# Loads of the first pairs, multiplies and the passage of a convolution and maxout kernel in another order

## The chip, the cores and the metric

The kernel runs on one NeuronCore of a Trainium2 chip. The metric is the time of one execution on the device, in microseconds (us). Before the change it is 2294.14 us, the median of three runs (2293.34 to 2296.65).

## The reference

A long convolution feeds a feed-forward block with three parallel input products. Shapes: B = 4 batches, S = 12544 positions, D = 128 channels, 50176 tokens in all, 768 hidden units; everything is float32.

```python
h_mlp = np.maximum(pos_emb @ w1, 0.0) @ w2
h_filt = h_mlp * np.exp(-0.01 * np.arange(S))[:, None]
u = x * v
Uf = np.fft.rfft(u, n=2 * S, axis=1)
Hf = np.fft.rfft(h_filt, n=2 * S, axis=0)
y = np.fft.irfft(Uf * Hf[None], n=2 * S, axis=1)[:, :S, :]
t = (x * y).reshape(B * S, D)
h = np.maximum(np.maximum(t @ moe_w1, t @ moe_w2), t @ moe_w3)
out = h @ moe_w_out
```

## The kernel before

The Fourier transform is done as products with small tables on TensorE (PE), in three steps. A first step takes 32 units of four channels each (`unit`, line 427, through `u_first`, L413) and leaves a spectrum of 90 columns in one large buffer, `spec`. A second step goes through 45 pairs of columns: each pair is transformed, multiplied with the spectrum of the filter, and transformed back half way. The results are rows, kept in device memory as `zd`. The third step belongs to the output: a tile of four positions per channel loads its rows (`t_load`), adds and subtracts their two halves (`t_sums`), and multiplies them with the table f4p and with x (`t_last`).

The instructions stand in the order in which the program text issues them (the schedule is manual). Each engine takes its own instructions strictly in that order, and so does SP, the engine that issues most of the DMAs. A DMA also waits until the DMA that stood eight places earlier in its queue has landed, because eight completion counters are used in turn.

**Three stages.** The opening (0 to about 308 us) convolves batch 0 and makes the filter. The middle (to about 1830 us) computes the feed-forward block of batch b - 1 and, beside it, the convolution of batch b, for b = 1, 2, 3. The end does the feed-forward block of batch 3 alone.

**The middle** counts time in slots. A batch has NT = 32 output tiles of NF = 6 hidden blocks, so 192 slots, each about 2.7 us of PE work. `conv_steps(b, done)` gives every step of the convolution a slot, and the main loop runs the steps of a slot after that slot's own work. Within one slot the loop first does `up` (two products into the banks hps, a Relu on ACT at L745, a maximum on DVE at L748), then the z sums of a coming tile, then the steps.

A unit u of the convolution passes through five steps. `u_load` (SP) fetches x and v. `u_mul` multiplies them on GpSimd, which the profile calls POOL (L361). `u_planes` clears the padding of a planes tile on POOL (L381) and copies the product there on ACT (L382). `u_dma` transposes it by a DMA from SP (L388). `u_join` puts the halves together on ACT (L397). Then `unit` runs on PE. With s the slot of the join, the load stands at s - 9, the multiply at s - 6, the planes at s - 5 and the transpose at s - 4. For batch 1 the first six units are done in the opening, and slots below zero are not used; for batches 2 and 3 the first units start in the last slots of the batch before.

A pair g has two loads. `q_load` (L443) regroups the spectra `sq` of two pairs out of `spec`, from on-chip memory to on-chip memory, four DMAs of 128 KB each. `h_load` (L456) loads the filter rows `ht` of two pairs from `hd` in device memory, four DMAs of 256 KB each. `w_load` (L433) loads one table. `g_quarter` multiplies them on PE (L472 forward, L482 back), and `q_re` on DVE (L516) is the first to read `ht`. The first pairs start at slot 55 in batch 1 and at slot 59 in batches 2 and 3; loads start no earlier than slot 52 (`LOADS`), because their buffers take the place of the buffers of the first eight tiles, whose output stores (L833, on SP) must be issued first.

**The passage** is what this text calls 285 to 326 us, between the opening and the middle. In its loop a step s transforms pair s, makes filter s - 1 (`s_filter`, ACT copy L1050 into `ht`), stores filter s - 2 (`s_store`, POOL, L1056) and multiplies pair s - 2 with it (`g_re`, `g_im`; for pair 43 the last add, L559, is on POOL). Pairs 43 and 44 come together at s = 45. `g_unfold` (DVE, L566) gives the operand `ab` of `g_third` (PE), whose copy `zs` is stored to `zd` by SP (L579). Then come units 0 and 1 of batch 1, the product of two weight matrices (`fold`), the constants f4p and sign, weight differences `tw` on POOL (L1136), and the first two output tiles. The PSUM banks of units 0 and 1 and of two transposes are given out by `banks_of`; before, the two halves of unit 1 share one tile of two banks.

Of the kernel before, what the change touches and what calls it, by code (L numbers as in the profile page):

```python
# [10 lines left out]
FP32 = mybir.dt.float32  # L11
# [5 lines left out]
P = 128  # L17
# [74 lines left out]
def kernel(  # L92
# [15 lines left out]
    nc = tc.nc  # L108
    NG, _, _, B, NB = x.shape
# [4 lines left out]
    NK = N1 // 2  # L114
# [10 lines left out]
    zd = [dram.tile([N1, 2, 64, 256] if b == 0 else [N1, 2, 32, 2, 256], FP32, name=f"zd{b}")  # L125
          for b in range(B)]
# [4 lines left out]
    f4p_d = nc.inline_tensor(np.ascontiguousarray(f4p_t), name="f4p_const").ap()  # L131
# [3 lines left out]
    sign_d = nc.inline_tensor(sign.copy(), name="sign_const").ap()  # L135
# [446 lines left out]
    def conv_steps(b, done):  # L582


        out = []

        def at(slot, late, fn, *args):
            out.append((slot, late, len(out), fn, args))

        for u in range(4, done):
            at(2 * (u - 4), 1, unit, u)
        lead, low = (1, -NT * NF) if b > 1 else (6, 0)
        share = UNIT * (NU - done - 1)
        per_pair = (END - lead - 6) / (share + (NK + LATE) // 2 * 2 - 2)
        for u in range(done, NU):
            s = (u - done) * UNIT * per_pair + lead
            load_ = max(low, int(s) - 9)
            at(load_, 0, u_load, b, u)  # L600
            mul = max(load_ + 2, int(s) - 6)
            at(mul, 0, u_mul, u, nc.gpsimd)
            at(max(mul, int(s) - 5), 0, u_planes, u)
            at(max(mul + 1, int(s) - 4), 0, u_dma, u)
            at(int(s), 0, u_join, u)
            at(int(s + 1), 1, unit, u)
        s0 = int(share * per_pair + lead) + 6

        def start(x):
            return s0 + int(x // 2 * 2 * per_pair)  # L610

        load = [0.6] * (NT * NF)
        for x in range(NK + LATE):
            s = start(x)
            load[s] -= 1.2
            load[s + 1 + x % 2] += 1.4

        def emptiest(among, cost):
            s = min(among, key=lambda i: load[i])
            load[s] += cost  # L620
            return s

        plan = []
        busy = {start(x): 2 for x in range(NK + LATE)}
        for x in range(NK + LATE):
            busy.setdefault(start(x) + 1, 1)
        for i in range(NT - 1):
            s = i * NF
            last = min((3, 4, 2), key=lambda k: busy.get(s + k, 0))
            load[s + last] += 0.6  # L630
            if s <= s0:
                plan.append((0, 0, last))
                continue
            a = emptiest(range(s, s + 2), 0.7) - s
            plan.append((a, emptiest(range(s + a, s + max(a + 1, last - 1)), 0.7) - s, last))
        plan.append((3, 3, 4))

        for x in range(NK + LATE):
            s, odd = start(x), x % 2
            g, z = x if x < NK else None, x - LATE if x >= LATE else None  # L640
            at(s, 1, g_quarter, g, z)
            at(s + 1 + odd, 0, g_fold, g, z)
            at(max(s - 4, LOADS) if x > 2 else LOADS + x // 2, 0, w_load, x)
            if z is not None:
                at(s + 3 + odd, 0, g_store, b, z)
            if g is None:
                continue
            if g % 2 == 0:
                at(max(s - 4, LOADS), 0, q_load, g, min(2, NK - g))
                at(s - 1 if g > 2 else LOADS + 1 + g // 2, 0, h_load, g, min(2, NK - g))  # L650
            first = s + 2 + 2 * odd
            at(first, 0, q_swap, g, 0)
            at(first + 1, 0, q_swap, g, 64)
            last = start(x + LATE) - 1
            a = emptiest(range(first + 1, min(first + 3, last - 1) + 1), 0.7)
            at(a, 0, q_re, g)
            a = emptiest(range(a, min(first + 4, last - 1) + 1), 0.7)
            at(a, 0, q_im, g)
            two = sorted(emptiest(range(a + 1, last + 1), 0.55) for _ in range(2))
            for q in range(2):  # L660
                at(two[q], 0, q_unfold, g, q)
        slots = {}
        for s, _, _, fn, args in sorted(out, key=lambda r: r[:3]):
            slots.setdefault(s, []).append((fn, args))
        return slots, plan, s0
# [5 lines left out]
    LOADS = TP * NF + 4  # L671
    UNIT, END = 0.65, 178
    zts, xTs, gs, pos_, obs = ({} for _ in range(5))

    def t_load(b, i):
        zt = hp.tile([N1, 2, 512], FP32, tag="zt", name="zt", bufs=2)
        for c in range(2):
            if b == 0:
                nc.sync.dma_start(
                    zt[NK * c:NK * c + NK],  # L680
                    zd[b].rearrange("(g a) c t f -> g a c t f", a=2)[
                        :, :, c, 2 * i:2 * i + 2, :].rearrange("g a t f -> g a (t f)"))
                continue
            q, j = divmod(i, NT // 2)
            for a in range(2):
                nc.sync.dma_start(
                    zt[NK * c:NK * c + NK, a].rearrange("g (t f) -> g t f", t=2),
                    zd[b].rearrange("(g a) c t q f -> g a c t q f", a=2)[
                        :, a, c ^ (a & q), 2 * j:2 * j + 2, q, :])
        zts[b, i] = zt[:, 0], zt[:, 1]  # L690
        if i % 2:
            return
        xT = hp.tile([D, 2, 4, NB], FP32, tag="xT", name="xT", bufs=2)
        for c in range(GC):
            nc.sync.dma_start(xT[c * NG:(c + 1) * NG].rearrange("d i p n -> d (i p) n"),
                              x[:, 4 * i:4 * i + 8, c, b, :])
        xTs[b, i], xTs[b, i + 1] = xT[:, 0], xT[:, 1]
# [248 lines left out]
    for f in range(0, FO, 4):  # L946
        quad([hs[:, f + i] for i in range(4)], (f1h[:, 0], f1h[:, 1]), specH[:, :, :, f:f + 4])
        u, k = divmod(f // 4, 4)
# [11 lines left out]
    for u in range(0, NU, 2):  # L960
        t = uts.pop(u)
        for v in range(2):
            if u + 4 < NU:
                u_mul(u + 4 + v)
            at = 4 * (u + v)
# [18 lines left out]
    cps = pro.enter_context(tc.tile_pool(name="cps0", bufs=3, space=PSUM))  # L984
    gps = pro.enter_context(tc.tile_pool(name="gps", bufs=2, space=PSUM))
    sps = pro.enter_context(tc.tile_pool(name="sps", bufs=1, space=PSUM))
    def banks_of():
        for _ in range(2):
            yield gps.tile([P, 512], FP32, tag="g", name="ps1")[:]
        both = sps.tile([P, 1024], FP32, tag="h", name="ps1")  # L990
        for h in range(2):
            yield both[:, 512 * h:512 * h + 512]
        for pool, tag in ((cps, "cv"), (gps, "g")):
            yield pool.tile([P, 512], FP32, tag=tag, name="pst")

    free = banks_of()

# [56 lines left out]
    def s_store(g):  # L1054
        for c in range(2):
            nc.gpsimd.dma_start(  # L1056
                hd[g, 64 * c:64 * c + 64],
                hts[g][64 * c:64 * c + 64, c].rearrange("p k q d -> p (k q d)"))
# [13 lines left out]
    for s in range(NK + 3):  # L1072
        if s < NK:
            ws[s, 0] = wf[s]
            s_second(s)
            if s + 1 < NK:
                s_minus(s + 1)
            g_second(s)
            wf.pop(s)
            if s + 3 < NK:  # L1080
                wf[s + 3] = load_dir(s + 3, 0)
        if 1 <= s <= NK:
            g_swap(s - 1)
            s_filter(s - 1)
        if s >= 3:
            ws[s - 3, 1] = wi.pop(s - 3)
            g_third(s - 3)
            if s < NK:
                wi[s] = load_dir(s, 1)
        ready = [g for g in {NK: (s - 2, s - 1)}.get(s, (s - 2,)) if 0 <= g and s <= NK]  # L1090
        for g in ready:
            s_store(g)
            g_re(g)
            g_im(g, g == NK - 2)
        for g in ready:
            g_unfold(g)
        if s < NK:
            g_butterfly(s)

        if s in muls:  # L1100
            u_mul(muls[s])
        if s in turns:
            u_turn(turns[s])
        if s in loads:
            u_load(1, loads[s])
        if s == NK:
            unit(0)
            pl = sps.tile([P, 512], FP32, tag="pl", name="pl")
        if s == NK + 1:
            for f in range(2):  # L1110
                folding(f)
# [11 lines left out]
    hidp = ctx.enter_context(tc.tile_pool(name="hidp", bufs=3))  # L1123
    hp = ctx.enter_context(tc.tile_pool(name="hp", bufs=3))
    f4p = hp.tile([N1, 2, 2, NB // 2], FP32, name="f4p", bufs=1)
    nc.sync.dma_start(f4p[:], f4p_d)
    sign_t = hp.tile([N1, 1], FP32, name="sign", bufs=1)
    nc.sync.dma_start(sign_t[:], sign_d)
    tw = hp.tile([P, 4, NC, 64], FP32, name="tw", bufs=1)
    linx = hp.tile([D, 64], FP32, name="linx", bufs=1)  # L1130
    b11, b12 = wo_sb[:, 0:NC, 0:64], wo_sb[:, 0:NC, 64:128]
# [34 lines left out]
    for n, (b, i) in enumerate(tiles[:LAST]):  # L1166
# [13 lines left out]
        for f in range(NF):  # L1180
            s = i * NF + f
# [130 lines left out]
```

## Time and profile before

| what | value |
|---|---|
| median of three runs | 2294.14 us |
| profiled execution | 2290.28 us |
| its span | 2288.5 us |
| mean granted PE clock | 0.995 |
| busy: PE, DVE, ACT, POOL | 99%, 68%, 54%, 44% of the span |
| DMA | 411.15 MB, mean 180 GB/s |
| issue to landing, median: ht, sq, wt | 6.6, 6.9, 5.8 us |

The profile is of one execution. Its span runs from the first to the last instruction of the program, and the execution's own time is 1.8 us longer. All times within it are counted from the start of the span. A timeline row gives the start, the length, the engine, the line, the operation and its tiles, and in brackets how long the engine had been idle before and what released it. SPq is SP's queue: the length of a row there is the time in which SP issues, and the transfer lands later. Busy time of PE is that of pipelined matmuls with modelled ends, so a busy PE is not always a fast one.

### The profile page before, as it was taken

What the parts mean: (1) busy time and instruction counts of PE and PEld (TensorE: products, weight loads), DVE (VectorE), ACT (ScalarE), POOL (GpSimd) and SP (SyncE); (2) the same over time, 40 slices, a digit from 0 to 9 for tenths busy, and PEclk for the clock granted to TensorE, in tenths of its full rate; (3) what the DMA queues carried; (4) which work ended last, traced back from release to release, by engine and by line L of the source; (5) the groups of instructions that cost most, each with busy time, mean ns of one, the idle gap of its engine ahead of it and who ended that gap; (6) DMA issues with size and microseconds to landing.
All of it is one profiled execution on the core that took longest, in us unless ns stands there. A gap on an engine that the chain in (4) does not pass through costs nothing.

```text
span 2288.5 us, 70172 instructions
## 1 busy us (share of the span) xinstructions
PE 2254.5 (99%) x28383; PEld 1397.2 (61%) x28383; DVE 1545.8 (68%) x3108; ACT 1227.9 (54%) x2210; POOL 1004.3 (44%) x1209
## 2 busy tenths in 40 slices
PE   8999989999999999999999999999999999999998
PEld 7999857745555557755555557755555556666665
DVE  5588956657878756658888856658888854545443
ACT  2688845546666546546666646536666622222222
POOL 2044357513333347713333348713333326666666
PEclk9999999999999999999999999999999999999999
DMA  7779979789999789979999889968999832222221
GB/s 192 178 238 276 300 168 185 129 197 233 234 242 236 201 161 188 168 168 232 247 239 235 225 151 193 171 160 229 246 243 236 216 86 56 55 67 66 61 55 23
DMA packets 485567, 411.15 MB, mean 180 GB/s; under 512 B 341305, under 2 KB 387866, under 8 KB 485242
## 3 DMA queue, kind: packets, MB, share of 16 engines
q1 hardware_dynamic: 459778, 334.30, 65.5%
q0 software_dynamic: 24752, 70.65, 10.3%
q8 instruction: 223, 3.65, 0.7%
q10 hardware_dynamic: 712, 1.70, 0.3%
q14 instruction: 102, 0.84, 0.1%
HBM read 262.84 MB, written 84.67 MB: 152 GB/s over the span
## 4 chain that ended last, share of the span: by engine, by line
PE 94%; DMA 3%; issue 1%; SPq 1%; POOL 0%; ACT 0%; DVE 0%; POOLq 0%; ACTq 0%; DVEq 0%
PE hps L156 43%; PE ops L156 14%; PE ops L809 8%; PE cps L413 5%; PE ps L156 4%; PE cps L156 4%; PE cps L472 3%; PE ps L165 3%; PE cps L482 3%; PE cps L809 2%; PE sps L1045 2%; PE gps L1027 2%; PE last L156 1%; DMA zt<-zd 1%; DMA sq<-spec 1%
## 5 line engine op out<-in xcount | busy, mean ns | idle before, releaser
L156 PE MATMUL hps<-gt,w_sb 128*64 128x392 f32 x6144 | 1147.7, 495 | 2.0 <-ACT hid L745 1.9
L745 ACT ACTIVATE hid<-hps 128x392 f32<-128x392 f32 x768 | 382.2, 498 | 822.5 <-PE hps L156 794.6
L748 DVE TENSOR_TENSOR hid<-hid,hps 128x392 f32<-128x392 f32 x768 | 428.1, 558 | 433.7 <-PE hps L156 331.1
L156 PEld LDWEIGHTS hps<-gt,w_sb 128*64 128x64 f32 x6144 | 419.9, 137 | 420.3 <-issue 387.1
L524 POOL TENSOR_TENSOR cb<-cb,xs 128x512 f32<-128x512 f32 x135 | 175.2, 1297 | 458.2 <-DVE xs L521 362.9
L156 PE MATMUL ops<-hid,wo_sb 128*64 128x392 f32 x1728 | 358.1, 493 | 0.0
L497 DVE TENSOR_TENSOR cb<-cps,eo 128x512 f32<-128x512 f32 (+1 forms) x288 | 175.1, 649 | 72.8 <-ACT eo L494 72.8
L156 PEld LDWEIGHTS ops<-hid,wo_sb 128*64 128x64 f32 x1728 | 124.5, 137 | 160.2 <-issue 160.1
L763 POOL DMA_DIRECT2D out_dram<-ot x72 | 56.7, 787 | 287.5 <-ACT ot L761 212.3
L512 ACT ACTIVATE xs<-cb 32x512 f32<-32x512 f32 x270 | 169.5, 628 | 19.4 <-DVE cb L497 10.5
L513 ACT COPY xs<-cb 32x512 f32<-32x512 f32 x270 | 166.3, 616 | 3.2
L528 DVE TENSOR_TENSOR xs<-cb 128x256 f32<-128x256 f32 x270 | 143.1, 575 | 9.3 <-POOL cb L524 9.3
L413 PE MATMUL cps<-f1q,uT 98*64 98x90 f32 x3008 | 133.6, 241 | 1.8 <-ACT uT L397 1.2
L413 PEld LDWEIGHTS cps<-f1q,uT 98*64 98x64 f32 x3008 | 127.2, 137 | 11.6 <-ACT uT L397 4.4
L397 ACT COPY uT<-turned 98x512 uint16<-98x512 uint16 x180 | 127.5, 781 | 0.0
L505 POOL DMA_DIRECT2D zd<-cb x135 | 92.5, 685 | 64.1 <-DVE cb L497 61.2
L778 POOL TENSOR_TENSOR s<-hid 128x392 f32<-128x392 f32 x84 | 86.4, 1028 | 75.1 <-DVE hid L748 73.8
L425 DVE TENSOR_TENSOR spec<-cps,high 128x180 f32<-128x180 f32 x376 | 112.6, 341 | 6.4
L778 POOL TENSOR_TENSOR s<-hid,s 128x392 f32<-128x392 f32 x84 | 86.4, 1029 | 49.8 <-DVE hid L748 49.4
L156 PEld LDWEIGHTS cps<-f4p,even 90*64 90x64 f32 x1568 | 87.9, 138 | 30.2 <-issue 29.2
L423 DVE COPY high<-cps 128x180 f32<-128x180 f32 x188 | 89.9, 478 | 23.2 <-PE cps L413 21.8
L361 POOL TENSOR_TENSOR ut<-ut 128x392 f32<-128x392 f32 x90 | 92.2, 1024 | 29.2 <-DMA ut<-in_vr_dram 26.4
(148 smaller groups left out, 3490.7 us busy)
## 6 DMA issues: line engine op xcount, KB each, us to landing
ht<-hd SPq DMA_DIRECT2D x264, 256.0 KB, 6.6
wt<-wq_const SPq DMA_DIRECT2D x144, 256.0 KB, 5.8
zd<-cb POOLq DMA_DIRECT2D x135, 256.0 KB, 5.4
zt<-zd SPq DMA_DIRECT2D x384, 90.0 KB, 3.1
sq<-spec SPq DMA_DIRECT2D x264, 128.0 KB, 6.9
ut<-in_xr_dram SPq DMA_DIRECT2D x128, 196.0 KB, 4.0
ut<-in_vr_dram SPq DMA_DIRECT2D x128, 196.0 KB, 4.1
xT<-in_x_dram SPq DMA_DIRECT2D x256, 98.0 KB, 3.3
```

Of the source, the lines that this page charges most:

```text
L156: nc.tensor.matmul(out[64 * h:64 * h + 64], lhsT[:, 64 * h:64 * h + 64], rhs, start=start, stop=stop, skip_group_check=True)
L397: nc.scalar.copy(uts[u][:, 8 * (u % 2):8 * (u % 2) + 8].rearrange("n s r t -> n (s r t)").bitcast(U16).rearrange("n (s r t h) -> n h s r t ...
L413: nc.tensor.matmul(ps[64 * c:64 * c + 64, 256 * i + h * N1:256 * i + (h + 1) * N1], t[:, 2 * ((at + i) % 8) + h].rearrange("n r t -> n (r ...
L497: nc.vector.tensor_tensor(out=cb[:, a, lo:hi], in0=ps[0][:, lo:hi], in1=eo[:, lo:hi], op=op)
L512: nc.scalar.mul(xs[at:at + 32], xt[at + 32:at + 64], -1.0)
L513: nc.scalar.copy(xs[at + 32:at + 64], xt[at:at + 32])
L524: nc.gpsimd.tensor_tensor(out=xts[g], in0=xts[g], in1=xs[:], op=ALU.add)
L528: nc.vector.tensor_tensor(out=ab[:, q], in0=y[:, 0], in1=y[:, 1], op=(ALU.subtract, ALU.add)[q])
L745: nc.scalar.activation(h[:], pa[:, 0:N], Relu)
L748: nc.vector.tensor_tensor(out=h[:], in0=h[:], in1=pb[:, 0:N], op=ALU.max)
L778: nc.gpsimd.tensor_tensor(out=out[:], in0=a[:], in1=b[:], op=op)
L809: nc.tensor.matmul(ps[64 * c:64 * c + 64, 0:H2], w, rhs[:, H2 * c:H2 * c + H2], start=start, stop=True, skip_group_check=True)
```

## The change

Five edits are made.

1. `conv_steps`: the multiply moves from slot s - 6 to s - 7, and the planes stand at least one slot after it. The transpose stands one slot after the planes. For the first three units of batch 1 this changes slots: units 6 and 7 keep the multiply at slot 2 and get planes at 3 and transpose at 4 (before 2 and 3); unit 8 gets its multiply at slot 2 (before 3).
2. `conv_steps`: the filter rows of the first two loads (g = 0 and 2) are loaded at s - 1, as all later ones are. Before they stood at slots 53 and 54; now at 54 and 59 in batch 1 and at 58 and 63 in batches 2 and 3.
3. The first z tile is loaded in two parts: 43 of the 45 row pairs, then the last two.
4. `banks_of` gives the two halves of unit 1 different tiles.
5. In the passage, stores of filters 42, 43 and 44 stand one step earlier or ahead of the multiplications, and f4p and sign are loaded from POOL's queue instead of SP's.

```diff
-            mul = max(load_ + 2, int(s) - 6)
+            mul = max(load_ + 2, int(s) - 7)
             at(mul, 0, u_mul, u, nc.gpsimd)
-            at(max(mul, int(s) - 5), 0, u_planes, u)
-            at(max(mul + 1, int(s) - 4), 0, u_dma, u)
+            planes = max(mul + 1, int(s) - 5)
+            at(planes, 0, u_planes, u)
+            at(planes + 1, 0, u_dma, u)
...
-                at(s - 1 if g > 2 else LOADS + 1 + g // 2, 0, h_load, g, min(2, NK - g))
+                at(s - 1, 0, h_load, g, min(2, NK - g))
...
+    def load_rows(zt, i, c, lo, hi):
+        nc.sync.dma_start(
+            zt[NK * c + lo:NK * c + hi],
+            zd[0].rearrange("(g a) c t f -> g a c t f", a=2)[
+                lo:hi, :, c, 2 * i:2 * i + 2, :].rearrange("g a t f -> g a (t f)"))
+
...
-                nc.sync.dma_start(
-                    zt[NK * c:NK * c + NK],
-                    zd[b].rearrange("(g a) c t f -> g a c t f", a=2)[
-                        :, :, c, 2 * i:2 * i + 2, :].rearrange("g a t f -> g a (t f)"))
+                load_rows(zt, i, c, 0, NK if i else NK - 2)
...
+        if b == i == 0:
+            for c in range(2):
+                load_rows(zt, i, c, NK - 2, NK)
...
-        for _ in range(2):
-            yield gps.tile([P, 512], FP32, tag="g", name="ps1")[:]
-        both = sps.tile([P, 1024], FP32, tag="h", name="ps1")
-        for h in range(2):
-            yield both[:, 512 * h:512 * h + 512]
-        for pool, tag in ((cps, "cv"), (gps, "g")):
-            yield pool.tile([P, 512], FP32, tag=tag, name="pst")
+        for pool, tag, n in ((gps, "g", 1), (gps, "g", 1), (sps, "h", 2), (gps, "g", 1),
+                             (cps, "cv", 1), (gps, "g", 1)):
+            yield pool.tile([P, 512 * n], FP32, tag=tag, name="ps1")[:, 0:512]
...
+        for g in {NK - 2: (s - 2, s - 1), NK - 1: (s - 1,), NK: (s - 1,)}.get(s, (s - 2,)):
+            if 0 <= g and s <= NK:
+                s_store(g)
         for g in ready:
-            s_store(g)
             g_re(g)
...
-    nc.sync.dma_start(f4p[:], f4p_d)
+    nc.gpsimd.dma_start(f4p[:], f4p_d)
...
-    nc.sync.dma_start(sign_t[:], sign_d)
+    nc.gpsimd.dma_start(sign_t[:], sign_d)
```

## The prediction

> **What bounds the kernel.** I read the page first, then TensorE's waits, then the granted clock around each wait, then the queues that ended it. The page:
>
> ```profile
> span 2288.5 us, 70172 instructions
> PE 2254.5 (99%) x28383; PEld 1397.2 (61%) x28383; DVE 1545.8 (68%) x3108; ACT 1227.9 (54%) x2210; POOL 1004.3 (44%) x1209
> ```
>
> TensorE (PE) is busy in all but 34 us, so a change that adds no matmul can gain only from those 34 us and from time in which PE is busy but slow. The waits of PE (releaser, sum, count, longest) name the 34:
>
> ```profile
> PE cps L472 <- DMA sq<-spec: 7.9, 7, 3.0
> PE ps L156 <- DVE ab L566: 4.3, 1, 4.3
> PE hps L156 <- ACT hid L745: 1.9, 2, 1.0
> PE ps L413 <- DVE spec L425: 1.3, 1, 1.3
> ```
>
> The 7.9 us are waits for the spectra of the first pairs. By PE's timeline they lie at 469.68 (0.17), 482.91 (2.99) and 486.34 (0.94) in the convolution of batch 1, 1001.41 (1.69) and 1003.54 (0.24) in batch 2, 1517.89 (1.38) and 1519.70 (0.47) in batch 3. The other three rows are the passage (285 to 326 us). The busy table of short windows, with the columns PE, PEld, DVE, ACT, POOL, clock, DMA share, GB/s, shows what follows a wait:
>
> ```profile
> 483.40:486.81 3.41, 0.43 (x4) 0.22 (x4) 2.62 (x5) 0.01 (x1) 0.62 (x1) 1.00 1.01 218
> 486.81:490.22 3.41, 2.94 (x44) 2.33 (x44) 0.00 (x0) 0.00 (x0) 0.64 (x1) 0.50 1.19 199
> 490.22:493.64 3.42, 3.42 (x16) 1.26 (x14) 0.34 (x1) 0.50 (x1) 0.00 (x0) 0.50 1.03 250
> 1521.04:1524.46 3.42, 3.42 (x16) 1.24 (x12) 0.18 (x1) 0.76 (x2) 0.00 (x0) 0.50 0.73 166
> 302.49:305.90 3.41, 3.41 (x18) 2.24 (x18) 0.55 (x2) 1.31 (x5) 0.00 (x0) 0.50 0.47 132
> ```
>
> After an idle window PE runs at half clock for one or two more, so a wait costs more than its length.
>
> **What the skill says.** The Trainium skill, "TensorE: Matmul & The Clock Gate", section "What's actually happening": the clock is full or half, by activity in free-running windows of 3413 ns. The trace agrees in the length (3.41 and 6.83 us at 0.50). It drops to half after an idle window there; here a window with 2.08 of 3.42 us busy (299.07 on) was enough, and I use that. "DMA: Bandwidth & Descriptors", section "Issuing engines are not separate DMA queues": DMAs of all engines run on the same 16 DMA engines and interleave. This agrees: spectra issued alone at 464.43 landed 3.6 us later, spectra issued at 476.14 behind rows took some 9. "SBUF — State Buffer", section "Who interferes with whom": a VectorE (DVE) instruction with two SBUF inputs contends with a GpSimd (POOL) one that reads SBUF. In the passage the DVE add L559 took 1.73 us beside POOL's subtractions, 0.69 elsewhere.
>
> **Part A, the row loads ht of the first pairs** (3 batches, two loads of four DMAs each, 256 KB a DMA by the page's issues). SP's timeline before:
>
> ```profile
> 472.09 3.03 SPq L456 DMA_DIRECT2D ht<-hd  x4
> 476.14 3.30 SPq L443 DMA_DIRECT2D sq<-spec  x4
> ...
> 482.54 2.04 SPq L679 DMA_DIRECT2D zt<-zd  x2
> ```
>
> In the built order of batch 1 the second ht load goes behind the second sq load. By bytes from 463.9 on, ahead of the end of that sq load stand three wt (0.75 MB), two sq (1.0), one zt (0.18), one ht (1.0) and an output tile (0.2): 3.13 MB. At the 220 GB/s of this stretch that is 14.3 us, from the first landing's start near 466: landed at about 480.5, and PE comes at 482.91. The wait goes. What is late next: the first ht, at about 478.5, wanted by DVE at 479.56; and the third sq load, which stays near 495 as the DMA engines are full (1.01 to 1.19), wanted by PE at 503.55 less what was gained, about 496. Both just hold. In batches 2 and 3 both ht loads leave the front of the first sq load. Spectra are complete at 991.50 (DVE's last L425), the sq load issues then and lands within 6 us, at 997.5; PE comes at 1001.41. Gain: 7.9 - 0.17 = 7.7 us of waits; half-clock time, half of it lost: (2.94 + 3.42 + 3.42)/2 = 4.9. **A = -12.6**, bounds -13.5 and -5.5.
>
> **Part P, the passage.** Of the filter stores, the built order of POOL moves one: the store of filter 44 now stands ahead of POOL's add L559 of pair 43. It waits for ACT's ht copy, ending 289.45; the add moves from 287.03 to about 290.85 and ends at 292.1, which is when DVE's L566 needs it (292.47). The 4.3 us wait therefore stays (0, bounds +0.5 and -0.3; DVE's L559 now meets this add instead of the subtractions). The banks: the second half of unit 1 no longer shares a tile with the first, so the 1.3 us wait goes (-1.3), and the half clock of 302.49 loses its cause, worth at most 3.41/2 = 1.7 (I take -0.7). The z load in two parts costs two more issues on SP (up to 0.9 us each by the rows of zt) and starts 43 of 45 rows at 300.0 instead of 301.86; its second part waits for the last zd stores (landed 301.78), with the xT and the second z load behind it as before; ready near 305 instead of 306.4. It hides behind PE's folds until 308.86 before; with PE about 2 us earlier it just holds, but the second z tile (landed near 309.4, two sums of 0.69 us) then holds PE some 0.5 (+0.5). The f4p and sign loads cost SP nothing, since they stood inside its wait for the last zd store (299.61 to 301.78); on POOL two issues of 0.54 us delay the tw subtractions, which nobody needs before 336. **P = -1.5**, bounds -3.0 and +0.5.
>
> **Part C, the multiplies.** 93 muls of 1.02 us, none added. Many wait for their load already (POOL ut <- DMA), so a slot (2.7 us) earlier they wait longer, with sums, stores and memsets queued behind. PE has no wait on any of these between 330 and 464, so this is hidden: a transpose lands mostly 4 us or more before its join. The exception is the start of batch 1, where units 6 and 7 lose a slot of planes:
>
> ```profile
> 318.99 1.02 POOL L361 TENSOR_TENSOR ut<-ut 128x392 f32<-128x392 f32 x1
> 319.95 0.30 POOL L381 MEMSET planes<- 128x240 uint16 x1
> 320.21 1.03 POOL L361 TENSOR_TENSOR ut<-ut 128x392 f32<-128x392 f32 x1
> 321.17 0.30 POOL L381 MEMSET planes<- 128x240 uint16 x1
> 321.43 1.26 POOL L710 TENSOR_TENSOR even<-zt 90x512 f32<-90x512 f32 x1
> 322.76 1.27 POOL L710 TENSOR_TENSOR zt<-zt 90x512 f32<-90x512 f32 x1
> ```
>
> The built order after is three muls, both z sums, then the memsets. The third mul's load (issued 316.87, to landing up to 5.5; SP some 0.6 ahead of before) comes near 321.8, mul to 322.9, sums to 325.4, first memset to 325.7, transpose landed 3.7 to 3.9 us later at 329.5, two join copies of 1.43 together: unit 6 starts at 331.0, not 329.28. Behind the waiting join on ACT stand the next planes copy and the next hid, behind the waiting third mul on POOL the z sums and all memsets. The two ACT hid waits (1.9) disappear, so PE arrives at 327.4 and stands 3.6 us. Net +1.7, and such a stand brings one or two half-clock windows, 1.7 each (I take 2.4). **C = +4.1**, bounds -0.3 (early loads, no half clock) and +6.3.
>
> **Sum.** -12.6 - 1.5 + 4.1 = -10.0. The profiled execution took 2290.28 us (span 2288.5), 3.9 under the median of 2294.14; I take the difference off the median: 2284.
>
> **Rivals.** (1) It goes better: the loads land early and C is at its low end, P too: -12.6 - 3.0 - 0.3 = -15.9, 2278. For it: landings of 3.2 us occur. Against: two z sums stand ahead whatever lands. (2) Batch 1's wait stays, since the DMA engines and not the order set it (share 1.0 and over): only batches 2 and 3 gain, 3.78 + 1.7 = 5.5; -5.5 - 1.5 + 4.1 = -2.9, 2291. Against: 1.0 MB less stands ahead. (3) Slower: POOL, held by muls, brings memsets and so transposes late beyond the first units. Place: units 2 to 5 at the start of batch 3 (transpose issued 1351.74, up to 6.4 to landing, joined 1358.32), the first of batch 2 and unit 6. With slacks of 0.5 to 3.6 us, seven units, 5.4 us of lateness costs about 20, and half clocks 8.5: +28 - 14.1 = +14, 2308. It decides from about 4 us late. Against: the memset of unit 2 stays behind the same mul, and that transpose waits for SP's order, not for POOL. (4) The change does not do what it says: for the filter store that holds already, and it is in P.
>
> **Numbers.** Chances: main 0.55, (1) 0.15, (2) 0.18, (3) 0.07, others 0.05. About 0.2% (4.6 us) is what a measurement of this kernel can tell. Faster takes nearly all of main and (1) and a quarter of (2); slower is (3) and tails: 0.76, 0.15, 0.09. Range 2276 to 2293: A's and C's bounds, (1) and (2).
>
> **What would show it.** Right: L472 waits for sq near 0.2 us in all, full clock at those places, no L413 wait for L425 at the passage, the 4.3 us wait still there, and a new L413 wait for uT of 2 to 4 us at the first joined unit. Wrong: sq waits at the second or third quarter product of batch 1; L413 waits for uT at the starts of batches 2 and 3; a shorter L566 wait.

## The result and the profile after

The changed kernel takes 2296.11 us (median of 13 runs, 2291.99 to 2298.86) against 2294.14 us (13 runs, 2288.89 to 2299.3). The ratio is 1.0004, 95% interval 0.9994 to 1.0014: no difference. The forecast was 2284 with a range of 2276 to 2293, so the result lies 3 us above the range. The mechanism forecast for the row loads worked; a new wait, for which the forecast had at most 0.5 us, gave the gain back. The page:

```profile
span 2291.7 us, 70158 instructions
PE 2253.1 (98%) x28383; PEld 1398.6 (61%) x28383; DVE 1546.9 (68%) x3108; ACT 1228.7 (54%) x2210; POOL 1006.5 (44%) x1211
```

The sum of PE's busy time is as before. The waits of PE (releaser, sum in us, count, longest) show both halves of the story:

```profile
PE cps L156 <- DVE even L717: 13.0, 1, 13.0
PE ps L156 <- DVE ab L566: 4.3, 1, 4.3
PE cps L413 <- ACT uT L397: 3.9, 3, 2.7
PE cps L472 <- DMA sq<-spec: 0.4, 1, 0.4
```

The 7.9 us for sq have become 0.4. The wait behind L425 (1.3) and those for hid (1.9) are gone. The 4.3 us for L566 stand. In the first place stands a new wait of 13.0 us, for the first z sums of batch 1. The busy table of short windows (length, then PE, PEld, DVE, ACT, POOL, clock, DMA share, GB/s) shows the new wait, what follows it, and the old places in the convolutions:

```profile
303.78:307.20 3.42, 2.71 (x45) 1.82 (x42) 0.00 (x0) 1.09 (x4) 0.32 (x1) 1.00 0.07 26
...
317.44:320.85 3.41, 0.65 (x8) 0.49 (x10) 1.62 (x3) 0.00 (x0) 0.00 (x0) 0.50 0.20 52
320.85:324.27 3.42, 3.42 (x56) 3.42 (x56) 3.32 (x9) 0.00 (x0) 0.00 (x0) 0.50 0.13 37
324.27:327.68 3.41, 3.41 (x26) 1.74 (x24) 2.24 (x8) 0.50 (x1) 0.00 (x0) 0.50 0.83 205
...
344.74:348.16 3.42, 3.42 (x24) 1.78 (x22) 2.99 (x8) 2.69 (x5) 2.34 (x4) 0.50 1.19 165
...
498.35:501.76 3.41, 3.27 (x58) 1.91 (x58) 3.38 (x7) 1.20 (x3) 0.00 (x0) 1.00 1.07 215
1522.34:1525.76 3.42, 3.42 (x38) 1.56 (x38) 1.12 (x2) 0.67 (x2) 0.00 (x0) 1.00 1.06 236
```

The last two rows are full clock and a busy PE where the kernel before stood and then ran slowly. The first row is the key to the rest. From 303.78 to 307.20 the z load is the DMA traffic, and it moves 26 GB/s at a DMA share of 0.07: that is the share of one of the 16 DMA engines (1/16 is 0.06), as if one alone carried it. The middle rows are its after-effect, PE busy at half clock until 327.68. Of 0.65 + 3.42 + 3.41 = 7.5 us of busy time, half is lost: 3.7. The row of 344.74 is half clock once more, behind the wait of 2.7 us for the first joined unit: another 1.7.

SP's timeline of the passage, first the kernel before:

```profile
301.86 1.91 SPq L679 DMA_DIRECT2D zt<-zd  x2
...
305.89 5.88 SPq L679 DMA_DIRECT2D zt<-zd  x4
...
313.89 0.45 SPq L354 DMA_DIRECT2D ut<-in_xr_dram  x1
```

The same timeline of the changed kernel, and below it DVE's first z sum (the bracket is DVE's idle time and its releaser):

```profile
300.91 8.36 SPq L677 DMA_DIRECT2D zt<-zd  x4
...
313.61 10.50 SPq L677 DMA_DIRECT2D zt<-zd  x4
...
326.23 0.45 SPq L354 DMA_DIRECT2D ut<-in_xr_dram  x1
```

```profile
319.20 0.69 DVE L717 TENSOR_TENSOR even<-zt 90x512 f32<-90x512 f32 x1 [16.69 <-DMA zt<-zd]
```

The first z tile is complete 18.3 us after the first issue (300.91 to 319.20), where it took 4.6 (301.86 to 306.50). SP's next z loads take 10.5 us to issue instead of 5.9, and the first load of u behind them is issued 12.3 us later than before. The start of batch 1 on POOL therefore shifts too:

```profile
331.88 1.02 POOL L785 TENSOR_TENSOR s<-hid 128x392 f32<-128x392 f32 x1 [26.04 <-DMA ut<-in_vr_dram]
332.86 2.98 POOL L361 TENSOR_TENSOR ut<-ut 128x392 f32<-128x392 f32 x3
335.81 1.26 POOL L717 TENSOR_TENSOR even<-zt 90x512 f32<-90x512 f32 x1
337.15 1.28 POOL L717 TENSOR_TENSOR zt<-zt 90x512 f32<-90x512 f32 x1
338.37 0.54 POOL L381 MEMSET planes<- 128x240 uint16 x2
```

The order is the one forecast: three multiplies, two sums, then two memsets together. The loads of the front of batch 1's convolution, which before had the rows ht ahead of sq:

```profile
480.73 2.50 SPq L443 DMA_DIRECT2D sq<-spec  x4
...
484.44 1.83 SPq L677 DMA_DIRECT2D zt<-zd  x2
486.60 1.82 SPq L456 DMA_DIRECT2D ht<-hd  x4
488.46 2.48 SPq L443 DMA_DIRECT2D sq<-spec  x4
```

The first row load now stands behind the first sq load, and the second sq load ahead of the second row load (issued at 492.64).

Put side by side by the same matmul of PE's sequence, the two traces part and meet like this:

| matmul | before, us | after, us | after less before |
|---|---|---|---|
| the last filter's products, at the start of the passage (L1045, L1048) | 285.67 | 286.34 | +0.7 |
| first on the z sums (L156) | 308.86 | 319.94 | +11.1 |
| first joined unit of batch 1 (L413) | 329.28 | 343.88 | +14.6 |
| ahead of batch 1's first pair (L156) | 461.23 | 477.54 | +16.3 |
| quarter product at the old 2.99 us wait (L472) | 485.90 | 498.60 | +12.7 |
| past the half clock of batch 1 (L156) | 492.31 | 501.49 | +9.2 |
| first pair of batch 2 (L472) | 1003.11 | 1011.14 | +8.0 |
| past the half clock of batch 3 (L156) | 1524.53 | 1527.92 | +3.4 |
| span | 2288.5 | 2291.7 | +3.2 |

The opening leaves the changed kernel 0.7 us behind, which differs from execution to execution (in "passage" the same products stand at 288.46). The passage, with the first joined unit and the half clock behind it, costs 15.6 more, and the three convolutions give 12.9 back.

### The profile page after: what moved, and what is told of

It is laid out like the page before. It is cut to its first block, busy times and chain, and to the rows that moved or that the text cites. A ratio compares the mean times of both kernels' runs of the same rounds, so it can differ in the third digit from the quotient of the medians.

```text
span 2291.7 us, 70158 instructions
## 1 busy us (share of the span) xinstructions
PE 2253.1 (98%) x28383; PEld 1398.6 (61%) x28383; DVE 1546.9 (68%) x3108; ACT 1228.7 (54%) x2210; POOL 1006.5 (44%) x1211
## 4 chain that ended last, share of the span: by engine, by line
PE 96%; DMA 2%; SPq 1%; issue 1%; ACT 0%; DVE 0%; POOL 0%; POOLq 0%; ACTq 0%; DVEq 0%
PE hps L156 44%; PE ops L156 14%; PE ops L816 8%; PE cps L413 5%; PE cps L156 4%; PE ps L156 4%; PE cps L472 3%; PE ps L165 3%; PE cps L482 3%; PE cps L816 2%; PE sps L1048 2%; PE gps L1030 2%; PE last L156 1%; DMA zt<-zd 1%; PE pst L366 1%; DMA sq<-spec 1%
## 5 line engine op out<-in xcount | busy, mean ns | idle before, releaser
L156 PE MATMUL hps<-gt,w_sb 128*64 128x392 f32 x6144 | 1147.3, 495 | 0.0
L156 PEld LDWEIGHTS hps<-gt,w_sb 128*64 128x64 f32 x6144 | 420.3, 137 | 416.8 <-issue 385.3
L156 PE MATMUL ops<-hid,wo_sb 128*64 128x392 f32 x1728 | 357.6, 492 | 0.0
L156 PEld LDWEIGHTS ops<-hid,wo_sb 128*64 128x64 f32 x1728 | 124.2, 137 | 159.2 <-issue 159.0
L413 PE MATMUL cps<-f1q,uT 98*64 98x90 f32 x3008 | 134.8, 243 | 4.2 <-ACT uT L397 3.9
L413 PEld LDWEIGHTS cps<-f1q,uT 98*64 98x64 f32 x3008 | 128.8, 138 | 14.2 <-ACT uT L397 7.2
L425 DVE TENSOR_TENSOR spec<-cps,high 128x180 f32<-128x180 f32 x376 | 112.6, 341 | 6.5
L156 PEld LDWEIGHTS cps<-f4p,even 90*64 90x64 f32 x1568 | 88.7, 139 | 43.7 <-issue 28.6
L156 PE MATMUL cps<-f4p,even 90*64 90x49 f32 x1568 | 96.4, 221 | 13.0 <-DVE even L717 13.0
```

What stands on the lines that cost most here:

```text
L156: nc.tensor.matmul(out[64 * h:64 * h + 64], lhsT[:, 64 * h:64 * h + 64], rhs, start=start, stop=stop, skip_group_check=True)
L413: nc.tensor.matmul(ps[64 * c:64 * c + 64, 256 * i + h * N1:256 * i + (h + 1) * N1], t[:, 2 * ((at + i) % 8) + h].rearrange("n r t -> n (r ...
L425: nc.vector.tensor_tensor(out=spec[:, :, a, at:at + n], in0=v[:, 1], in1=high, op=op)
```

## The experiments

Every ratio is to runs of the kernel before beside it (medians 2294.19 to 2294.77).

**Theory Z**: the split of the z load costs, and it does so because 43 rows cannot be divided over the DMA engines, so that both loads of 43 rows go through one engine. **Rival S**: two parts cost, by their issues and by the wait for the last stores, whatever their rows. **Rival M**: something else of the passage, or the early multiplies, brings the z sums late.

### The load by itself (run "ladder")

```diff
     for at_ in sorted(stream):
         run(stream[at_])
+    zt = hp.tile([N1, 2, 512], FP32, tag="zt", name="zt", bufs=2)
+    for rows in (45, 44, 43, 42, 41, 40, 38, 36, 35, 32, 30, 16, 5, 2):
+        nc.sync.dma_start(zt[0:rows], ...)      # the form of load_rows, lo = 0, hi = rows
+        seen = hp.tile([N1, 512], FP32, tag="even", name="even", bufs=2)
+        nc.vector.tensor_copy(seen[0:rows, :], zt[0:rows, 0])
```

> The kernel before, and behind its last store fourteen loads from the spectra of batch 0 in the form of the z load, one at a time, with 45, 44, 43, 42, 41, 40, 38, 36, 35, 32, 30, 16, 5 and 2 rows of 4 KB; a VectorE copy reads each before the next is issued. They add time at the end; only the time from issue to landing of each is read. Theory Z (rows that don't divide over the DMA engines): a load is spread over as many of the 16 DMA engines as the largest divisor of its row count up to 16, and one engine moves about 25 GB/s, as in the window 304 to 307 of the changed kernel (25 to 27 GB/s at a DMA share of 0.06, one sixteenth). So 43 rows (172 KB) and 41 rows (164 KB) take 6.6 to 7 us of transfer and land 8 to 9 us after issue, 38 rows (two engines, 152 KB) about 5, 35 rows (seven engines) about 3, and 45, 44, 42, 40, 36, 32, 30, 16, 5 and 2 rows between 2 and 3 us. Rival S (the split itself is the cost, by its two more issues and the wait for the last stores): no count stands out; 45 to 40 rows land within 0.5 us of each other.

DVE's timeline at the end of this run. Each copy waits for its load alone, and the bracket is that wait:

```profile
2288.87 0.42 DVE L1283 COPY even<-zt 44x512 f32<-44x512 f32 x1 [3.85 <-DMA zt<-zd]
2298.93 0.42 DVE L1283 COPY even<-zt 43x512 f32<-43x512 f32 x1 [9.64 <-DMA zt<-zd]
2302.93 0.42 DVE L1283 COPY even<-zt 42x512 f32<-42x512 f32 x1 [3.58 <-DMA zt<-zd]
2312.44 0.42 DVE L1283 COPY even<-zt 41x512 f32<-41x512 f32 x1 [9.09 <-DMA zt<-zd]
2316.32 0.42 DVE L1283 COPY even<-zt 40x512 f32<-40x512 f32 x1 [3.47 <-DMA zt<-zd]
2322.52 0.42 DVE L1283 COPY even<-zt 38x512 f32<-38x512 f32 x1 [5.78 <-DMA zt<-zd]
2326.39 0.42 DVE L1283 COPY even<-zt 36x512 f32<-36x512 f32 x1 [3.45 <-DMA zt<-zd]
2330.40 0.42 DVE L1283 COPY even<-zt 35x512 f32<-35x512 f32 x1 [3.60 <-DMA zt<-zd]
...
2345.30 0.41 DVE L1283 COPY even<-zt 2x512 f32<-2x512 f32 x1 [2.19 <-DMA zt<-zd]
```

Loads of 43 and 41 rows take 9.6 and 9.1 us, one of 38 takes 5.8, and 44, 42, 40, 36 and 35 rows take 3.5 to 3.9. One row more or less decides. The busy table of the stretches inside four of these transfers (of 43, 42, 41 and 38 rows) names the cause, in its last two columns:

```profile
2292.00:2298.00 6.00, 0.00 (x0) 0.00 (x0) 0.00 (x0) 0.00 (x0) 0.00 (x0) 0.50 0.07 26
2301.00:2302.50 1.50, 0.00 (x0) 0.00 (x0) 0.00 (x0) 0.00 (x0) 0.00 (x0) 0.50 0.33 108
2306.00:2311.50 5.50, 0.00 (x0) 0.00 (x0) 0.00 (x0) 0.00 (x0) 0.00 (x0) 0.50 0.07 26
2319.50:2322.00 2.50, 0.00 (x0) 0.00 (x0) 0.00 (x0) 0.00 (x0) 0.00 (x0) 0.50 0.12 44
```

43 and 41 rows hold a share of 0.07 at 26 GB/s, 38 rows 0.12 at 44 GB/s: one engine and two. Rival S has no place for this. The expectation had the order right and the times somewhat low: 8 to 9 us against 9.6 and 9.1, about 5 against 5.8, and for 44 to 36 rows 2 to 3 against 3.5 to 3.9. From 32 rows down a load took 2.2 to 2.9. Thirty-five rows, seven engines by the theory, cannot be told from 36.

The Trainium skill states the rule: "DMA: Bandwidth & Descriptors", section "Why a DMA increments its semaphore by 16 and not by 1". A DMA takes the largest number of engines up to 16 that divides the slowest dimension of both sides, and from a queue such as SP's these are the lowest-numbered ones. By it 43 and 41 rows get one engine, 38 two, 45 fifteen. The ladder agrees for one and two. That the engines are the lowest-numbered would put both loads of 43 rows on the same one: the first window of the changed kernel (0.07, with both of them issued) fits that, and so does the length, 2 x 172 KB (352,000 bytes) at 26 GB/s, 13.5 us.

### One part, and other rows (runs "whole", "split40", "split38", "before43")

The first load in one part again, in the changed kernel:

```diff
-                load_rows(zt, i, c, 0, NK if i else NK - 2)
+                load_rows(zt, i, c, 0, NK)
...
-        if b == i == 0:
-            for c in range(2):
-                load_rows(zt, i, c, NK - 2, NK)
```

> The changed kernel with its first z load in one part for each half again, 45 rows as before; all else as changed. Theory Z and rival S (the split): TensorE's wait of 13.0 us for the z sum goes to under 1, and with it the half clock from 310.61 to 327.68, in which PE was busy from 320 on (about 7 us, half of it lost, 3.6) and the SP queue behind it comes back, so that the wait of 2.7 us for the first joined unit is at most 3.6 as forecast: 2296 - 13 - 3.6 = 2279, between 2276 and 2283. Rival M (the multiplies, the f4p load on POOL or the banks bring the passage late): the wait stays over 8 us, the time over 2290.

2282.67 us (6 runs), ratio to before 0.9953 (0.9936 to 0.997): 13.4 us under the changed kernel by the medians, 11.7 by the two ratios. PE's waits and the windows after the z sums:

```profile
PE cps L413 <- ACT uT L397: 4.1, 3, 2.9
...
PE cps L156 <- DVE even L714: 1.0, 1, 1.0
```

```profile
305.76:309.18 3.42, 2.47 (x43) 1.75 (x41) 0.20 (x1) 0.85 (x4) 0.32 (x1) 1.00 0.75 182
309.18:312.59 3.41, 2.29 (x50) 1.86 (x52) 3.31 (x9) 0.00 (x0) 0.00 (x0) 1.00 0.61 156
312.59:316.00 3.41, 3.41 (x24) 2.05 (x26) 3.31 (x9) 0.50 (x1) 0.00 (x0) 0.50 0.48 131
```

The wait of 13.0 is 1.0, and one window at half clock stands there in place of five. Rival M falls. The split is the cost; which property of it, the next run tells.

```diff
-                load_rows(zt, i, c, 0, NK if i else NK - 2)
+                load_rows(zt, i, c, 0, NK if i else NK - 5)
...
-                load_rows(zt, i, c, NK - 2, NK)
+                load_rows(zt, i, c, NK - 5, NK)
```

> The changed kernel with its first z load in two parts of 40 and 5 rows in place of 43 and 2. Theory Z: 40 rows spread over 10 engines, the z tile is there by 307, and the time is that of the load in one part within 2 us (2277 to 2283). Rival S (two parts cost, whatever their rows): the wait for the z sum stays over 8 us and the time over 2290.

2282.04 us (6 runs), ratio 0.9947 (0.9929 to 0.9965). Two parts of 40 and 5 rows cost nothing against one part that these runs can tell (each interval is some 4 us to either side). Rival S falls: it is the count of rows.

```profile
315.01 0.69 DVE L717 TENSOR_TENSOR even<-zt 90x512 f32<-90x512 f32 x1 [4.50 <-DMA zt<-zd]
```

A gain cannot be told from the times either, but the trace shows that this split does what it was made for. Its first part is issued at 309.22, 0.5 us behind the last zd store (308.76, landed 2.1 us later). In "whole" the load is issued at 304.13, when that store (301.86, 2.1 us as well) has landed. Counted from the issue of the store, the first z sum starts 6.3 us later here and 7.1 us later in "whole" (at 308.98): some 0.9 us are won, and PE waits 0.8 us in place of 1.0.

With 7 in place of 5, 38 rows and two engines:

> The changed kernel with its first z load in parts of 38 and 7 rows. Theory Z (as many DMA engines as the largest divisor up to 16 of the row count): 38 rows go over two engines, 152 KB a load. Alone such a load took 5.8 us to its reader, where 40 rows took 3.5. If both loads of 38 rows fall on the same two engines, 304 KB at 2 x 24 GB/s take 6.3 us, and the z sum comes some 9 us after the first issue, where it came 5.8 after it with 40 and 5 rows: PE waits 4 us for it in place of 0.8, with up to 2 of half clock more, 2285 to 2288, between the 2282.0 of 40 rows and the 2296.1 of 43. If they fall on different engines, 1 to 2 us later than with 40 rows, 2283 to 2284. Rival (43 and 41 rows are special, or two parts are): as with 40 rows, or as with 43.

2287.43 us (5 runs), ratio 0.997 (0.9958 to 0.9981), between the other two and inside the range given for a shared pair of engines. PE waits for the z sums:

```profile
PE cps L156 <- DVE even L717: 5.2, 1, 5.2
```

5.2 us, where 4 were expected: the z sum came 11.1 us after the first issue (301.65 to 312.74), not 9. So the delay follows the largest divisor of the row count up to 16, which by the theory is the number of engines: 0.8 us of wait at ten, 5.2 at two, 13.0 at one.

And the split alone in the kernel before:

```diff
-                nc.sync.dma_start(
-                    zt[NK * c:NK * c + NK],
+                for lo, hi in ((0, NK),) if i else ((0, NK - 2), (NK - 2, NK)):
+                    nc.sync.dma_start(
+                        zt[NK * c + lo:NK * c + hi],
...
```

> The kernel before with one edit: the first z load goes in parts of 43 and 2 rows, both in place of the old load. Theory Z: two loads of 172 KB on one engine, 344 KB at 25 GB/s = 13.8 us where it took 4.5 to 5: the z sum comes 9 to 13 us late, half clock follows (3 to 6), and SP's queue with the loads of batch 1 stands behind it: 2294 + 12 to 19, about 2309. Rival S gives the same here. Rival M: within 3 us of 2294.

2309.37 us (4 runs), ratio 1.0067 (1.0048 to 1.0086): +15 us (11 to 20), with all else as before.

```profile
PE cps L156 <- DVE even L711: 11.2, 1, 11.2
PE cps L472 <- DMA sq<-spec: 9.7, 6, 3.1
```

The z wait appears with 11.2 us, and the waits for sq are there as in the kernel before.

### The other parts alone (runs "rows_only", "mul_only", "passage", "whole_nomul")

```diff
-                at(s - 1 if g > 2 else LOADS + 1 + g // 2, 0, h_load, g, min(2, NK - g))
+                at(s - 1, 0, h_load, g, min(2, NK - g))
```

> The kernel before with one edit: the row loads of the first pairs of each batch are placed like those of the others (part A alone). Theory A (as forecast): the waits for sq at the first quarter products go from 7.9 to about 0.2 us and the half clock behind them goes, -12.6: 2294.2 - 12.6 = 2281.6, between 2279 and 2284; no half-clock window between 330 and the end of the span but the last. Rival (the DMA engines and not the order set batch 1's wait): the waits at 483 and 486 stay, only -5.5, 2288.7.

2279.31 us (5 runs), ratio 0.9938 (0.9926 to 0.995), which is -14.2 us with an interval of -17 to -11.5. The DMA engines do not keep batch 1's wait.

```profile
PE cps L472 <- DMA sq<-spec: 1.1, 2, 0.8
```

No half-clock window is left between 308 and 2274; the 1.1 us are two waits at 498 and 499, at the third sq load of batch 1, behind the place of the old ones.

The multiplies alone (the first hunk of the change):

> The kernel before with one edit: the multiply of a unit two slots ahead of its planes (part C alone). As forecast: +4.1, 2298.3, with a wait of PE of about 3.6 for the first joined unit of batch 1 and one or two half-clock windows behind it, the two waits for hid (1.9) gone. By the profile of the changed kernel with its z load whole, where the same stretch cost 2.0 (waits for hid gone, 1.6; wait for the joined unit 2.9; half clock 1.0 or so): 2296.2. Rival (hidden, as a multiply is 1 us on an engine that is busy less than half the time): 2294.2 within 1.5, no new wait.

2298.12 us (13 runs), ratio 1.0009 (0.9999 to 1.002): +2 us, -0.2 to +4.6. By the ratio alone this is not told from zero, but the new wait is there:

```profile
PE cps L413 <- ACT uT L397: 4.5, 3, 3.2
...
PE hps L156 <- ACT hid L746: 0.8, 1, 0.8
```

3.2 us at the first joined unit, and one wait for hid less. The half clock that the forecast added behind it did not come in this run.

The passage without the split, rows and multiplies as before:

> The kernel before with the passage's edits but the split: filter stores moved up, banks separate, the f4p and sign loads on POOL; row loads and multiplies as before. Forecast, without the z load's terms: -1.3 for the wait behind L425 and -0.7 for the half clock at 302: 2292.2. By the profile of the changed kernel with its z load whole, PE gains these 2.0 and then stands 1.4 for the z sums, which nothing brought forward, with half a window of half clock (1.2) behind it: 2294.8, no difference. In both the wait of 4.3 us for L566 stays within 0.5.

2294.22 us (14 runs), ratio 0.9998 (0.9989 to 1.0008). The waits that take the place of those removed:

```profile
PE cps L156 <- DVE even L713: 1.4, 1, 1.4
```

Counted from the last filter's products, PE comes to the products ahead of the z sums about 3 us earlier (288.46 to 307.20 here, 285.67 to 307.57 before). It then stands 1.4 us for the z sums and 0.4 for the second of them, and a window of half clock follows (3.41 us of the granted clock, from 311.90). It balances.

The changed kernel without split and early multiplies:

> The changed kernel with its z load in one part and the multiplies at their old places: the passage's banks, stores and constants and the row loads are left. If the multiplies cost 2.0 to 4.1: 2282.7 less that, 2278.6 to 2280.7. If they cost nothing: 2282.7 within 1.5. If they help somewhere in the three convolutions: over 2284.

2278.28 us (5 runs), ratio 0.9933 (0.992 to 0.9946), 4.4 us under "whole". The two intervals overlap, so the times alone do not settle it. The traces agree with such a cost of the multiplies beside the other edits: from the last filter's products to the first joined unit PE takes 43.3 us here (287.94 to 331.24) and 45.1 in "whole" (287.75 to 332.86), and only in "whole" does a window of half clock follow, worth up to 1.7.

### The multiplies without their start (run "whole_planes")

"whole", with this edit:

```diff
-            planes = max(mul + 1, int(s) - 5)
+            planes = max(mul, int(s) - 5)
             at(planes, 0, u_planes, u)
-            at(planes + 1, 0, u_dma, u)
+            at(max(mul + 1, int(s) - 4), 0, u_dma, u)
```

> The changed kernel with its z load in one part, the multiplies a slot early as changed, but the planes of a unit whose multiply is held by its load stay in the multiply's slot, and its transpose a slot behind it, as in the kernel before; this differs in units 6 and 7 of batch 1 alone. As forecast (all that the early multiplies cost lies at the start of batch 1): the wait for the first joined unit goes from 2.9 us to under 0.5 and the time from 2282.7 to that of the old multiplies, 2278.3 within 1.5. Rival (the early multiplies cost, or give, something in the three convolutions): no nearer than half way, 2280.5 or more; or under 2276.5.

2276.55 us (6 runs), ratio 0.9928 (0.9915 to 0.9941): 6.1 us under "whole", 0.3 us lower than expected and just short of the 2276.5 at which the rival, that the early multiplies give something, would have had it. PE's waits:

```profile
PE cps L156 <- DVE even L714: 1.4, 1, 1.4
...
PE cps L413 <- ACT uT L397: 1.2, 2, 0.6
```

The wait at the first joined unit is gone; the 1.2 that remain are the two of 0.6 at the starts of batches 2 and 3, which the kernel before has as well. So what the early multiplies cost lies, as far as these runs can tell, in units 6 and 7 of batch 1, and this version has the lowest time of all that ran, 0.7% under the kernel before. Its intervals overlap those of "rows_only" and "whole_nomul", so what the early multiplies themselves give cannot be told.

## Why the prediction was wrong

| term | forecast, us | measured alone | by the waits and windows of after |
|---|---|---|---|
| A, row loads | -12.6 | -14.2 (-17 to -11.5) | -7.5 of waits, -4.9 of half clock |
| P, banks, stores, constants, without the split | -1.5 with it | -0.5 (-2.5 to +1.8) | -1.3 of waits, -1.7 of half clock |
| P, the split of the z load | 0 to +0.5 | +15 in the kernel before, +11.7 to +13.4 in the changed one | +13.3 of waits, +3.7 of half clock |
| C, multiplies | +4.1 | +2 (-0.2 to +4.6), +4.4 beside the rest (intervals overlap) | -1.9 and +2.7 of waits, +1.7 of half clock |

The 13.3 are 13.0 for the first z sum and 0.3 for the second. The last column sums to +4.1, and the opening adds 0.7, against 3.2 of the spans. The other 1.6 are not placed: that half of the busy time is lost at half clock is an estimate.

**The step that failed** is in part P: "It hides behind PE's folds until 308.86 before; with PE about 2 us earlier it just holds", with the z tile "ready near 305 instead of 306.4". It priced 43 rows like 45, by bytes, and counted only the two more issues. The load of 43 rows ran on one DMA engine, and the z sum began at 319.20. The row "zt<-zd ... 90.0 KB, 3.1" median of the issues gave no hint, since all z loads of the kernel before have 45 rows. Had this term been sized at its 12 to 13 us, the forecast would have been about 2297, and the result is 2296.11. That the rest fits so well (2284 forecast, 2282.67 for "whole") may be in part luck: in the runs of single parts, part A gave 1.6 us more than forecast and part P without the split 1 us less, and each forecast still lies within the interval measured. No rival held it either: the slower one was placed on POOL.

**What held.** Part A by its steps: the second sq load was in time, the third all but "just holds", and no half clock is left in the convolutions. One wait of 0.4 us stands at the third load (1.1 in "rows_only"), which is by the prediction's own list a sign of being wrong, though a small one. The rival that the DMA engines keep batch 1's wait was wrong. In the passage the wait for L425 went and the wait of 4.3 us for L566 stood, as said. In part C the order on POOL, the wait at the first joined unit (2.7 us after, 3.6 forecast) and the end of the waits for hid came as said, and no wait for uT appeared at the starts of batches 2 and 3 beyond the old 0.6. What part P saved at the banks turned into a wait for the z sums even without the split ("passage"): the forecast had 0.5 for that, the run shows 1.8 and a window of half clock.

**Smaller slips of the prediction.** Its four lines of PE's waits do not name the 34 us: they sum to 15.4. It counts 93 multiplies, where POOL's timeline before has 90. The two spectra loads it compares (3.6 us alone, some 9 behind rows) were both issued by SP, so they show that loads delay each other, and not that those of other engines do. None of this bears on the result.

## What to carry to other kernels

Price a DMA by how many engines it gets, not by its bytes alone: cut a load so that the row count of each part keeps a large divisor up to 16, and look at the DMA share of the window in which it runs, where 0.06 to 0.07 means one engine. With enough engines, as in parts of 40 and 5 rows, the split brought the z sum some 0.9 us forward, which is too little to see in the time. When a total shows no difference, line the two traces up by the same instructions: here a loss of 16 us before 350 us and gains of 13 from 469 us on nearly cancelled, and the loss could be taken out by itself.

## What was not expected of the hardware

- One engine moves 26 GB/s in this form of load (rows of 2 KB pieces), two move 44 (run "ladder"). A load of 43 rows takes 9.6 us, of 42 rows 3.6.
- A load on one engine delays others: the x tiles issued behind it, which took 3.0 to 3.2 us to land before, took up to 10.0. By the rule quoted above they have a share on that engine, and the trace fits this: when the two loads of 43 rows were through, what was left of the x tiles moved at the share of one engine, almost all of it in packets under 512 B.

```profile
318.40:320.10 1.70, 0.16 (x4) 0.16 (x4) 0.87 (x2) 0.00 (x0) 0.00 (x0) 0.50 0.07 20
```

- The clock falls without an idle window, but not after every gap, and PE's busy time in the window does not decide it alone. In "whole" a window with 2.47 of 3.42 us busy was followed by full clock and the next one, with 2.29 of 3.41, by half clock. In "passage" two windows with 1.64 and 1.95 us busy both kept full clock, and so did the one behind them (1008.23 to 1011.64). What else decides it stays open.

```profile
1001.40:1004.81 3.41, 1.64 (x10) 0.41 (x6) 0.56 (x1) 0.50 (x1) 0.00 (x0) 1.00 0.95 204
1004.81:1008.23 3.42, 1.95 (x36) 1.41 (x38) 0.00 (x0) 0.00 (x0) 0.00 (x0) 1.00 0.86 172
```
